# Two more blocks of the first token span in split products, with a new order table

## The chip, the cores and the metric

The kernel runs on one core of one Trainium2 chip. The metric is the time of one execution on the device in microseconds; three runs of the kernel before gave 891.29, 891.6 and 891.9 us.

## The reference

The reference is an attention with linear cost, followed by a gated feed-forward layer, all in fp32. With B = 8, H = 8, S = 576 tokens and D = 64 the second part sees 4608 tokens of width 512, and DF = 1536.

```python
q_s = exp(q - max(q, axis=-1));  q_s = q_s / (sum(q_s, axis=-1) + 1e-9)
k_s = exp(k - max(k, axis=2));   k_s = k_s / (sum(k_s, axis=2) + 1e-9)
kv  = einsum('bhsd,bhse->bhde', k_s, v)
x   = einsum('bhsd,bhde->bhse', q_s, kv)       # then tokens x (heads * D)
out = (sigmoid(x @ w_gate) * (x @ w_val)) @ w_out
```

The two input weight matrices come as `w_in`, cut into 12 blocks of 128 columns of each, the output weights as `wo`, in 12 blocks of 128 rows. Both arrive as 64-bit floats and are narrowed to fp32 on the chip, in four steps that the names `w_top`, `w_low`, `w_sign`, `w_join` (and `wo_...`) stand for: ScalarE converts the upper words, VectorE shifts the lower ones, ScalarE casts the sign, VectorE joins the bits.

## The kernel before, in words

The tokens are taken in nine spans of 512. In spans 1 to 8 (`g1`, `g2`) the product with `w_in` goes over six pairs of blocks, in a scheme with seven products for each 2x2 of sub-blocks; its right sides are the weights of a pair, kept on the chip as `a_w`, and four sums of their parts, kept in memory as `s`. Each fp32 number there is split in a high and a low part of fewer bits (`fp32r`), and a product is the sum of high x high, high x low and low x high.

The first span is another: here the weights are still being read, narrowed, summed (`w_sums`, `sums_keep`) and split (`split_hi` on ScalarE, `split_lo` on VectorE) while the span is computed block by block. For block j, `g1_0(j)` makes gate and value into two PSUM banks, `g_sig_0` and `g_mul_0` make h from them, and `g2_0(j)` multiplies h with the output block into four accumulators. Blocks 0 to 5 take `g1_0` in plain fp32 from the narrowed weights `f_w` and `x_0`; blocks 6 to 11 take it as split products from `a_w`, `a_21` and `x_hl`. `g2_0` is plain fp32 for blocks 0 to 4 and split for 5 to 11 (`in_parts`), with `h_hi_0` and `h_lo_0` for h and `wo_hi`, `wo_lo` for the output weights. An output block is stored for the later spans in both parts (`wo_store`, 512 KB) or, where `wo_late` says so, whole (`wo_keep`, 256 KB), and is then split in the second span (`wo_load` into a staging tile, `wo_split`, and a store).

Beside the blocks of the first span runs the attention for the second: the maxima of batch 1's keys (`k_max_turn` on TensorE, `k_max_send`, `k_max_read`), their subtraction (`k_sub`, five instructions `ring<-ring,kmax_b` on VectorE), exponentials, `k_mm`, and the like for the queries. `k_max_send` is a copy on ScalarE into `kmax_b` and a small transfer of 2 KB to memory (`kmax_row`); `k_max_read` is a transfer that spreads the row over 128 partitions, back into `kmax_b`. Both are issued by GpSimd, the second when the first has landed. Loads are issued by SyncE.

Every engine works off its own instructions in the order in which the program wrote them. From the first load to the start of span 2's second pair that order isn't the code's: the class `Steps` keeps the calls under the name of their step, and `put(ORDER)` writes them out as the table `ORDER` lists them (the line of all of these is then L89; L87 is the line of a call outside the table). What waits for what follows from the tiles that the instructions share.

Of the kernel before, what the change touches and what calls it, by code (L numbers as in the profile page):

```python
# [99 lines left out]
qf_tr.0.0 q_sum_0.2:1 qT_copy.0 q_sum_0.2:2 qf_tr.0.1 top:15 top:16 qT_copy.1 k_done_0 k_done_0:1 w_top.0.1  # L100
qf_mul.0.2 x_mm_0.0 kv_split.0:2 qf_mul.0.3 x_ev_0.0 w_low.0.0 qf_tr.0.2 x_mm_0.1 qT_copy.2 top:17 w_low.0.1
top:18 qf_tr.0.3 x_mm_0.2 qT_copy.3 w_join.0.0 x_mm_0.3 x_ev_0.2 x_ev_0.1 wo_top.0 w_top.1 wo_low.0 x_ev_0.3
wo_sign.0 w_join.0.1 w_low.1 split_hi.0 w_sign.1 split_lo.0 w_join.1 g1_0.0 g_sig_0.0 wo_join.0 wo_top.1
w_sums.0 load_wo.3 load_w.4 k_load.1.3 w_top.2 g_mul_0.0 wo_low.1 kv_split.0:3 w_sums.0:1 w_low.2 top:19
w_sign.2 x_split_hi.0 g1_0.1@4 g_sig_0.1 w_sums.0:2 w_top.3 g1_0.1 k_max_turn.1 g_mul_0.1 wo_hi.0 w_join.2
wo_sign.1 wo_top.2 qn_max.1.0 kv_split.0 w_low.3 g2_0.0 wo_low.2 w_sign.3 wo_join.1 qn_sub.1.0 load_wo.4
kT_load.2.1 k_load.1.1 v_load.1.1 wo_sign.2 k_load.1.4 load_w.5 qn_max.1.3 k_max_send.1 qn_max.1.2
k_max_send.1:1 qn_max.1.1 wo_join.2 qn_sub.1.2 g1_0.2@4 g_sig_0.2 load_wo.5 k_load.1.2 v_load.1.0 load_w.6
k_load.1.0 w_join.3 k_max_read.1 sums_keep.0 qn_sub.1.3 k_sum.1.3 load_w.7 x_split_lo.0 g1_0.2 k_sum.1.0
wo_top.3 qn_sub.1.1 wo_hi.1 wo_low.3 kv_split.0:1 k_sum.1.1 wo_lo.0 w_top.4 g2_0.1 x_split_hi.1 w_low.4  # L110
top:20 qn_exp.1.3 qn_exp.1.0 qn_sum.1.3 split_hi.1:1 g_mul_0.2 split_hi.0:1 k_sub.1.1 wo_sign.3 k_sum.2.0
wo_join.3 w_sign.4 w_sums.0:3 wo_keep.3 load_wo.6 v_load.1.4 v_load.1.2 v_load.1.3 qn_sum.1.0 sums_keep.0:1
w_sums.1 split_hi.1 wo_store.0 wo_lo.1 g1_0.3 w_join.4 wo_store.1 wo_top.4 sums_keep.0:3 k_sum.1.2 k_sub.1.4
sums_keep.1 load_w.8 qn_exp.1.2 sums_keep.0:2 wo_low.4 w_top.5 qn_sum.1.2 wo_keep.2 top:21 g2_0.2 qn_exp.1.1
# [1628 lines left out]
```

## Time and profile before

| | |
|---|---|
| median of three runs | 891.6 us |
| profiled execution, its time | 891.47 us |
| its span in the trace | 889.7 us |
| TensorE busy | 880.2 us (99%) |
| VectorE busy | 710.5 us (80%) |
| ScalarE busy | 592.1 us (67%) |
| GpSimd busy | 174.5 us (20%) |
| granted clock of TensorE, mean | 0.998 |

The span is what the trace shows from the first to the last instruction; 1.8 us of the execution's time lie around it. Shares are means over stages with different limits: what a change in one stage is worth is read from that stage.

### The profile page before, as it was taken

To read this page: it belongs to the slowest core of one execution; us is meant where nothing else is said; L and a number is where in the kernel's file an instruction comes from. 1 tells how busy PE (TensorE), PEld (TensorE's weight loads), DVE (VectorE), ACT (ScalarE), POOL (GpSimd) and SP (SyncE) were. 2 spreads that over 40 slices of the span, in tenths; PEclk is the share of its full clock that TensorE was granted. 3 is DMA by queue.
4 is the path that set the end of the run, shared out by engine and by line. 5 is a ranking of instruction groups with operands and counts; after the bars stand their busy time and mean duration, and the time that the engine had idled before them with its cause. 6 is when DMAs were issued, how large, how long until landed. Compare 5 with 4: busy or idle time off the path is not lost.

```text
span 889.7 us, 17035 instructions
## 1 busy us (share of the span) xinstructions
PE 880.2 (99%) x6533; PEld 800.6 (90%) x6533; DVE 710.5 (80%) x1126; ACT 592.1 (67%) x1006; POOL 174.5 (20%) x326
## 2 busy tenths in 40 slices
PE   8999999999999999999999999999999999999998
PEld 7445889999999999999999999999999999999997
DVE  7889999978797788868887888878877787886553
ACT  5889877776585767676676668556856664764432
POOL 0021221312112212121212122112211212122220
PEclk9999999999999999999999999999999999999999
DMA  9798657786787579774987499648965578535441
GB/s 332 283 390 303 242 194 227 239 265 198 260 256 224 179 226 283 231 215 143 331 243 238 123 321 295 176 156 287 300 177 165 155 217 247 164 121 190 145 141 71
DMA packets 75657, 199.16 MB, mean 224 GB/s; under 512 B 12636, under 2 KB 12920, under 8 KB 74168
## 3 DMA queue, kind: packets, MB, share of 16 engines
q0 software_dynamic: 31888, 109.60, 39.3%
q1 hardware_dynamic: 43688, 88.47, 30.8%
q8 instruction: 51, 0.84, 0.4%
q14 instruction: 30, 0.25, 0.1%
HBM read 174.98 MB, written 23.05 MB: 223 GB/s over the span
## 4 chain that ended last, share of the span: by engine, by line
PE 80%; DVE 8%; DMA 7%; issue 3%; ACT 1%; POOL 0%; SPq 0%; DVEq 0%; ACTq 0%; POOLq 0%
PE gv L87 44%; PE acc L87 25%; PE gv L89 5%; PE acc L89 3%; DMA s<-s 2%; PE at L87 2%; DMA kmax_b<-kmax_row 1%; DMA out<-x 1%; DVE ring L89 1%; DMA s_sb<-s 1%; DVE s L89 1%; DMA lent<-q_in 1%; PE at L89 1%; DVE f_w L89 1%; DMA kmax_row<-kmax_b 1%
## 5 line engine op out<-in xcount | busy, mean ns | idle before, releaser
L87 PE MATMUL gv<-c_hl,s_sb 128*128 128x256 f32 x1968 | 234.1, 275 | 0.1
L87 PEld LDWEIGHTS gv<-c_hl,s_sb 128*128 128x128 f32 x1968 | 226.8, 192 | 0.4 <-DVE s_sb L87 0.3
L87 ACT COPY sg<-gv 128x512 f32<-128x512 f32 x164 | 96.1, 586 | 138.1 <-PE gv L87 136.7
L87 PE MATMUL gv<-c_hl,a_w 128*128 128x256 f32 x1476 | 185.1, 275 | 0.0
L87 PEld LDWEIGHTS gv<-c_hl,a_w 128*128 128x128 f32 x1476 | 174.8, 192 | 0.1
L87 POOL DMA_DIRECT2D s_sb<-s x160 | 86.6, 541 | 260.7 <-PE gv L87 196.1
L87 DVE TENSOR_TENSOR s_sb<-s_sb 128x512 fp32r<-128x512 f32 x162 | 106.2, 686 | 31.9 <-ACT s_sb L87 31.8
L87 DVE TENSOR_TENSOR sg<-sg 128x512 f32<-128x512 f32 (+1 forms) x123 | 70.1, 598 | 66.6 <-ACT sg L87 66.6
L87 PEld LDWEIGHTS acc<-wo_t,h 128*128 128x128 f32 x548 | 103.3, 189 | 14.6
L87 PE MATMUL acc<-wo_hl,h 128*128 128x512 f32 x504 | 116.2, 380 | 0.0
L87 PE MATMUL acc<-wo_t,h 128*128 128x512 f32 (+1 forms) x548 | 115.9, 362 | 0.0
L87 ACT CAST s_sb<-s_sb 128x512 fp32r<-128x512 f32 x162 | 98.1, 624 | 6.9 <-DMA s_sb<-s 6.4
L87 PEld LDWEIGHTS acc<-wo_hl,h 128*128 128x128 f32 x504 | 92.1, 189 | 11.6
L87 DVE TENSOR_TENSOR sg<-gv,sg 128x512 f32<-128x512 f32 (+1 forms) x123 | 73.7, 599 | 26.7 <-PE gv L87 25.3
L87 ACT ACTIVATE sg<-sg 128x512 f32<-128x512 f32 x82 | 38.4, 514 | 38.7 <-DVE sg L87 38.6
L87 DVE TENSOR_TENSOR h<-sg,h 128x1024 fp32r<-128x1024 f32 x41 | 50.3, 1226 | 1.4
L87 POOL DMA_DIRECT2D wo_hl<-wo x40 | 21.5, 536 | 149.9 <-PE acc L87 149.9
L87 ACT ACT_TABLE_LOAD x34 | 43.6, 1283 | 0.6
L89 PE MATMUL gv<-x,f_w 128*128 128x512 f32 x96 | 42.1, 593 | 0.0
L89 PE MATMUL gv<-c_hl,s_sb 128*128 128x256 f32 x336 | 40.9, 277 | 1.2 <-ACT sg L89 0.9
L87 ACT ACTIVATE ring<-ring 128x512 f32<-128x512 f32 (+1 forms) x73 | 41.0, 622 | 0.1
L89 PEld LDWEIGHTS gv<-c_hl,s_sb 128*128 128x128 f32 x336 | 39.1, 192 | 1.7 <-ACT sg L89 1.1
(207 smaller groups left out, 1244.1 us busy)
## 6 DMA issues: line engine op xcount, KB each, us to landing
s_sb<-s POOLq DMA_DIRECT2D x184, 256.0 KB, 4.9
wo_t<-wo POOLq DMA_DIRECT2D x45, 512.0 KB, 4.6
wo_hl<-wo POOLq DMA_DIRECT2D x44, 512.0 KB, 3.7
out<-x SPq DMA_DIRECT2D x35, 256.0 KB, 4.9
ring<-k_in SPq DMA_DIRECT2D x28, 256.0 KB, 8.6
ring<-qn_in SPq DMA_DIRECT2D x28, 256.0 KB, 5.0
ring<-qT_in SPq DMA_DIRECT2D x28, 256.0 KB, 5.8
q_b<-q_m_row SPq DMA_DIRECT2D x56, 128.0 KB, 6.9
```

Source lines behind the costliest of these rows:

```text
L87: do(*args, **kw)
L89: self.steps.keep(self.name, lambda: do(*args, **kw))
```

## The change

Blocks 4 and 5 of the first span take gate and value as split products, and block 4's output product is split too. For that pair 2's weights are split before their use instead of after it, and in block 5's case a third part (`THIRD`, the tile `a_21`) is made. Output block 4 is stored in both parts, blocks 0 and 1 are kept whole and split in the last step of the second span, staged in the two tiles of `v_two`. The table `ORDER` is another in nearly all of its lines and goes on for one more pair of span 2.

```diff
     def wo_late(j):
-        return 2 <= j <= 4
+        return j < 4
...
             if w == 1 and wo_late(j):
-                wo_stage[j] = x = kmax_b if i else f_last[:, 3].rearrange("p n e -> p (n e)")
+                wo_stage[j] = x = v_two[i] if p == 0 else kmax_b if i else f_last[:, 3].rearrange("p n e -> p (n e)")
...
     def in_parts(j):
-        return j >= 5
+        return j >= 4
...
-                if j < 6:
+                if j < 4:
                     pairs = [(w[:, kt // 2, sl], x_0[:, kt])]
...
-    splits = {2: (0, FIRST, LAST), 4: (1, FIRST, LAST), 5: (2, FIRST, LAST)}
+    splits = {2: (0, FIRST, LAST), 4: (1, FIRST, LAST)}
...
         ahead = ()
-        if j >= 5:
+        if j >= 3:
             ahead = (FIRST,) if j % 2 else (THIRD, LAST)
         split_hi((j + 1) // 2, ahead)
...
-            if (w, at) == (2, 1):
+            if (w, at) == (2, 2):
                 nc.put(ORDER)
...
-            if w == 1 and at == 3:
-                wo_split(w, p)
-            if w == 1 and at == 4:
+            if w == 1 and at in (4, 5):
                 wo_split(w, p)
...
-qn_exp.1.1 qn_max.1.2 k_max_send.1:1 qn_max.1.1 wo_join.2 qn_sub.1.2 g1_0.2@4 g_sig_0.2 load_wo.5 k_load.1.2 v_load.1.0 load_w.6
+qn_exp.1.1 qn_max.1.2 k_max_send.1:1 wo_top.3 split_lo.1 sums_keep.0:3 qn_exp.1.0 k_sum.1.2 qn_sub.1.2
```

**First place: blocks 3 to 5 on TensorE.** Before, from block 3's gate and value to the key products behind block 4's output product (`f_w` are fp32 weights, `acc` the output, `at` the key products):

```order
L89 MATMUL gv<-x_149,f_w 128x512 x8
L89 MATMUL acc<-wo_t,h_228 128x512 x4
L89 MATMUL gv<-x_149,f_w 128x512 x8
L89 MATMUL acc<-wo_t,h_235 128x512 x4
L89 MATMUL gv<-x_149,f_w 128x512 x8
L89 MATMUL acc<-wo_t,h_247 128x512 x4
L89 MATMUL at<-v_115,ring 64x64 x8
```

The same stretch of the changed kernel:

```order
L89 MATMUL gv<-x_149,f_w 128x512 x8
L89 MATMUL acc<-wo_t,h_226 128x512 x4
L89 MATMUL gv<-x_hl,a_w 128x512 x24
L89 MATMUL acc<-wo_t,h_233 128x512 x4
L89 MATMUL gv<-x_hl,a_245 128x512 x6
L89 MATMUL gv<-x_hl,a_w 128x512 x6
L89 MATMUL gv<-x_hl,a_245 128x512 x6
L89 MATMUL gv<-x_hl,a_w 128x512 x6
L89 MATMUL acc<-wo_hl,h_parts 128x512 x12
L89 MATMUL at<-v_115,ring 64x64 x8
```

Two times eight fp32 products became two times 24 split ones, and block 4's four output products became twelve; the rest of TensorE's order in the first span is as before.

**Second place: the key maxima on ScalarE.** Before, the copy into `kmax_b` stands behind the sign cast of weight block 3 (`x_112<-f_w`) and of output block 1:

```order
L89 ACTIVATE wo_t<-wo_raw 128x512
L89 CAST kv_sb<-f_last 64x4x64
L89 CAST x_112<-f_w 128x2x512
L89 CAST wo_raw<-wo_t 128x2x256
L89 COPY kmax_b<-at 4x128
L89 ACTIVATE h_228<-gv 128x512
```

Now it stands behind the sigmoid of block 2 (`h_226`), the sign casts of weight blocks 4 and 5 (one row, x2) and two exponentials of keys (`lent,k_sum`):

```order
L89 ACTIVATE h_226<-gv 128x512
L89 ACT_TABLE_LOAD
L89 ACTIVATE lent,k_sum<-lent,k_neg 128x576
L89 ACTIVATE f_w<-w_raw 128x1024
L89 CAST w_raw<-f_w 128x2x512 x2
L89 ACTIVATE lent,k_sum<-lent,k_neg 128x576
L89 COPY kmax_b<-at 4x128
```

It moved behind seven instructions that came after it or were elsewhere before. On VectorE, the subtraction that needs the result came, before, behind these rows (the first of them ends when the copy on ScalarE has been made for some time):

```order
L89 TENSOR_TENSOR x_hl<-x_149,x_hl 128x1024
L89 TENSOR_TENSOR ring<-ring,q_m 128x512
L89 TENSOR_SCALAR wo_raw<-wo_raw 128x2x256
L89 TENSOR_TENSOR kv_sb<-f_last,kv_sb 64x4x64
L89 TENSOR_TENSOR wo_hl<-wo_t,wo_hl 128x512
L89 TENSOR_SCALAR w_raw<-w_raw 128x2x512
L89 TENSOR_REDUCE k_neg<-kt_117 128x1
L89 TENSOR_REDUCE q_r<-ring 128x8
L89 TENSOR_TENSOR h_228<-gv,h_228 128x512
L89 TENSOR_TENSOR ring<-ring,kmax_b 128x512
```

Now these stand between the shift of block 5's words (`TENSOR_SCALAR w_raw<-w_raw`, with one row `TENSOR_TENSOR a_w<-f_w,a_w 128x512` behind it, both just ahead of the first row here) and the subtraction:

```order
L89 SCALAR_TENSOR_TENSOR f_w<-f_w,w_raw 128x1024
L89 TENSOR_TENSOR h_226<-gv,h_226 128x512
L89 TENSOR_REDUCE q_m<-ring 128x8
L89 TENSOR_TENSOR a_w<-f_w,a_w 128x2x512
L89 TENSOR_TENSOR ring<-ring,q_m 128x512
L89 TENSOR_SCALAR wo_raw<-wo_raw 128x2x256
L89 TENSOR_REDUCE q_r<-ring 128x8
L89 SCALAR_TENSOR_TENSOR f_w<-f_w,w_raw 128x1024
L89 TENSOR_TENSOR s_254<-f_w 128x512
L89 TENSOR_TENSOR a_w<-f_w,a_w 128x2x512
L89 TENSOR_TENSOR a_w<-f_w,a_w 128x512
L89 TENSOR_TENSOR ring<-ring,kmax_b 128x512 x2
```

The subtraction has kept its place among the steps of block 3, while the copy on ScalarE that it depends on went back behind weight block 5's cast.

**Third place: GpSimd's queue.** The two transfers of the maxima were the first in it; now it begins with stores of weight sums (`s_121`, `s_122`) and of output block 0 (`wo_127`):

```order
L89 DMA s_121<-s_211 128x512
L89 DMA wo_127<-wo_t 128x512
L89 DMA s_122<-s_243 128x512
L89 DMA s_121<-s_209 128x512
L89 DMA kmax_row<-kmax_b 4x128
L89 DMA s_121<-s_212 128x512
L89 DMA kmax_b<-kmax_row 128x512
L89 DMA wo_128<-wo_t 128x512
```

Four stores went ahead of the row, one between the two, and the store of output block 1 stands behind.

## Rows read from the trace of the kernel before

**Rows 1.** Busy time by stage: window, length, then busy us (instructions) by engine.

```profile
core 0: us, PE busy (x) PEld busy (x) DVE busy (x) ACT busy (x) POOL busy (x), PEclk, DMA share, GB/s
25.00:62.70 37.70, 37.70 (x90) 16.57 (x89) 32.48 (x48) 31.39 (x47) 5.10 (x9) 1.00 0.87 325
62.70:86.60 23.90, 23.90 (x134) 11.77 (x132) 23.66 (x37) 22.67 (x30) 3.84 (x8) 1.00 0.85 312
86.60:143.50 56.90, 56.18 (x283) 48.08 (x280) 53.64 (x84) 45.93 (x66) 11.55 (x19) 1.00 0.70 240
143.50:260.00 116.50, 115.36 (x924) 110.29 (x925) 97.93 (x159) 82.96 (x143) 25.82 (x48) 1.00 0.74 231
```

**Rows 2.** Timeline of TensorE: start us, busy us, merged instructions, first span.

```profile
42.13 7.03 PE L89 MATMUL gv<-x,f_w 128*128 128x512 f32 x16
48.99 3.60 PE L89 MATMUL acc<-wo_t,h 128*128 128x512 f32 x8
52.43 7.03 PE L89 MATMUL gv<-x,f_w 128*128 128x512 f32 x16
...
80.02 3.60 PE L89 MATMUL acc<-wo_t,h 128*128 128x512 f32 x8
...
86.58 5.43 PE L89 MATMUL gv<-x_hl,a_w 128*128 128x512 f32 x24
91.84 2.75 PE L89 MATMUL acc<-wo_hl,h_parts 128*128 128x512 f32 x12
94.44 0.79 PE L89 MATMUL at<-ring,kv_sb 128*128 128x64 f32 x5
...
96.15 1.69 PE L89 MATMUL gv<-x_hl,a 128*128 128x512 f32 x6
...
101.56 2.99 PE L89 MATMUL acc<-wo_hl,h_parts 128*128 128x512 f32 x12
```

**Rows 3.** Chain that ended last (start, us); then quickest landings, 100 to 200 us.

```profile
44.28 5.12 DMA kmax_row<-kmax_b
...
49.70 7.18 DMA kmax_b<-kmax_row
...
158.28 4.30 DMA kmax_b<-kmax_row
...
DMA to landing us min/median/max: 3.3/3.9/4.4
```

**Rows 4.** VectorE: timeline, groups by form (count, mean ns), and its waits.

```profile
26.36 0.69 DVE L89 COPY x<-acc 128x512 f32<-128x512 f32 x1
...
35.07 2.54 DVE L89 TENSOR_REDUCE k_neg<-lent 128x4 f32<-128x2304 f32 x1
...
56.90 0.69 DVE L89 TENSOR_TENSOR ring<-ring,kmax_b 128x512 f32<-128x512 f32 x1 [1.81 <-DMA kmax_b<-kmax_row]
57.51 0.69 DVE L89 SCALAR_TENSOR_TENSOR wo_t<-wo_t,wo_raw 128x512 int32<-128x512 int32 x1
58.11 0.69 DVE L89 TENSOR_TENSOR s<-f_w,s 128x512 f32<-128x512 f32 x1
...
60.51 1.22 DVE L89 SCALAR_TENSOR_TENSOR f_w<-f_w,w_raw 128x1024 int32<-128x1024 int32 x1
61.65 0.68 DVE L89 TENSOR_TENSOR ring<-ring,kmax_b 64x512 f32<-64x512 f32 x1
...
L89 DVE TENSOR_SCALAR wo_raw<-wo_raw 128x512 uint32<-128x512 uint32 x6 | 2.5, 422 | 1.6 <-ACT wo_t L89 1.6
...
DVE s L89 <- DMA s<-s: 2.4, 3, 1.2
...
DVE a_w L89 <- ACT a_w L89: 0.5, 1, 0.5
```

**Rows 5.** Timeline of ScalarE, with idle time ahead of a row and its releaser.

```profile
17.04 0.68 ACT L89 ACTIVATE f_w<-w_raw 128x512 f32<-128x512 f32 x1 [1.85 <-DMA w_raw<-w_in]
...
43.74 0.24 ACT L89 COPY kmax_b<-at 4x128 f32<-4x128 f32 x1
...
47.67 0.78 ACT L89 ACTIVATE lent<-lent,k_neg 128x576 f32<-128x576 f32 x1
...
66.02 1.36 ACT L89 CAST w_raw<-f_w 128x1024 f16<-128x1024 f32 x1
```

More of the change, by code (lines that the diff above doesn't have):

```diff
@@ L100 @@
[L100 to L114, printed above, removed]
@@ L190 @@
[L190 to L194 removed]
+top:7 load_w.3 load_wo.2 qn_load.1.0 qn_load.1.1 qn_load.1.2 qn_load.1.3 top:8 top:10 top:9 top:11 k_sum.0.0
@@ new lines @@
+top:17 qT_copy.3 w_join.0.0 x_ev_0.0 x_mm_0.3 x_ev_0.2 w_join.0.1 w_top.1 x_ev_0.3 load_w.4 x_split_hi.1
+w_low.1 wo_low.0 x_split_lo.1 wo_sign.0 w_sign.1 split_hi.0 w_join.1 w_sums.0:2 load_w.5 w_sums.0 g1_0.0
+sums_keep.0:2 g_sig_0.0 w_sums.0:1 w_top.2 w_sums.0:3 x_split_hi.0 wo_join.0 w_low.2 wo_keep.0 load_wo.3
+k_load.1.0 g_mul_0.0 top:19 g1_0.1@4 g_sig_0.1 w_sign.2 split_lo.0 w_top.3 g1_0.1 wo_top.2 w_low.3
+k_max_turn.1 wo_low.2 w_sign.3 w_join.2 split_hi.0:1 w_join.3 load_w.6 k_load.1.3 kv_split.0 g2_0.0
@@ new lines @@
+qn_max.1.0 split_hi.1:1 qn_max.1.1 wo_top.1 qn_max.1.3 wo_sign.2 wo_low.1 split_hi.1 wo_join.2 qn_sub.1.0
+wo_sign.1 load_wo.5 k_load.1.2 g_mul_0.1 w_top.4 wo_join.1 g1_0.2@4 g_sig_0.2 split_lo.1:1 load_wo.4
+v_load.1.0 k_load.1.1 k_load.1.4 kT_load.2.0 load_w.7 kT_load.2.1 v_load.1.4 v_load.1.2 w_low.4 v_load.1.3
+qn_sub.1.1 k_sum.1.1 qn_sub.1.3 g1_0.2 w_top.5 w_sums.1:2 x_split_lo.0 sums_keep.1:2 w_sign.4 sums_keep.0
+w_low.5 split_lo.0:1 w_sign.5 w_join.4 g2_0.1 k_sum.1.3 g_mul_0.2 load_w.8 v_load.1.1 k_max_send.1
@@ new lines @@
+split_lo.2.6.5 wo_keep.2 wo_low.5 top:20 k_exp.1.4 qn_sum.1.0 g1_0.4 wo_sign.5 k_sub.1.1 k_exp.1.3
+w_sums.1:1 k_exp.1.2 wo_join.5 k_exp.1.0 wo_join.4 kv_split.0:2 g2_0.3 qn_sum.1.3 wo_hi.4 w_join.6 k_sum.2.0
+w_top.7 qn_sum.1.3:1 load_w.9 w_sums.1:3 load_wo.8 load_wo.7 load_w.10 g_mul_0.4 sums_keep.1:3 k_exp.1.1
+w_sums.2 wo_keep.3 h_hi_0.4 kv_split.0:1 wo_hi.5 sums_keep.1:1 w_low.7 sums_keep.2 wo_lo.4 sums_keep.2:2
+w_sign.7 h_lo_0.4 g1_0.5 k_done.1:1 top:21 split_hi.3.0 qn_sum.1.3:2 qf_mul.1.0 k_sum.2.1 split_lo.3.0
@@ new lines @@
+g2_0.4 wo_lo.5 k_mm.1.0 g_sig_0.5 w_join.7 k_mm.1.1 k_mm.1.2 g_mul_0.5 k_mm.1.3 k_mm.1.4 h_hi_0.5 k_done.1:2
+qf_tr.1.0 w_sums.2:1 kv_split.1:2 kv_split.1 kv_split.0:3 sums_keep.2:1 split_hi.3.6.5 qf_mul.1.1 wo_store.4
+split_hi.3.6.5:1 w_sums.3 wo_top.6 w_sums.2:3 qT_split.1.0 h_lo_0.5 sums_keep.2:3 g1_0.6@12 g_sig_0.6
+qT_split.1.0:1 wo_store.5 w_top.8 kv_split.1:3 split_lo.3.6.5 g1_0.6 wo_low.6 w_sums.3:1 wo_sign.6
+kv_split.1:1 w_top.9 qf_mul.1.3 split_lo.3.6.5:1 g2_0.5 wo_join.6 w_low.8 x_mm.1.0@4 qn_load.2.0 x_mm.1.0
@@ new lines @@
+load_wo.9 qf_tr.1.1 qf_mul.1.2 w_sign.8 w_sums.3:2 g_mul_0.6 x_ev.1.0 sums_keep.3:2 w_low.9 h_hi_0.6
+w_join.8 g1_0.7@12 g_sig_0.7 wo_hi.6 w_sums.3:3 load_w.11 qT_split.1.1 wo_lo.6 sums_keep.3:3 wo_top.7
+sums_keep.3 qT_split.1.1:1 g1_0.7 wo_top.8 wo_store.6 wo_low.7 w_top.10 h_lo_0.6 sums_keep.3:1 g_mul_0.7
+split_hi.4.0 g2_0.6 wo_sign.7 split_lo.4.0 w_sign.9 x_mm.1.1 wo_low.8 qf_tr.1.2 w_low.10 h_hi_0.7 w_join.9
+qT_split.1.2 wo_join.7 w_sums.4:2 load_wo.10 g1_0.8@12 g_sig_0.8 qT_split.1.2:1 wo_hi.7 split_hi.4.6.5
@@ new lines @@
+wo_lo.7 wo_sign.8 h_lo_0.7 g1_0.8 x_ev.1.1 g_mul_0.8 wo_join.8 qn_max.2.0 load_wo.11 wo_hi.8 k_load.2.0
+qn_load.2.2 kT_load.2.3 qn_load.2.1 kT_load.2.2 w_sums.4 wo_top.9 g2_0.7 split_lo.4.6.5 sums_keep.4
+split_hi.4.6.5:1 w_sums.4:1 x_mm.1.2 wo_store.7 h_hi_0.8 qf_tr.1.3 split_lo.4.6.5:1 sums_keep.4:2
+qT_split.1.3 w_sums.4:3 x_ev.1.2 wo_lo.8 w_sign.10 sums_keep.4:3 sums_keep.4:1 wo_low.9 qn_sub.2.0
+wo_store.8 wo_sign.9 w_join.10 g1_0.9@12 g_sig_0.9 w_top.11 h_lo_0.8 qT_split.1.3:1 split_hi.5.0 g1_0.9
@@ new lines @@
+c_subs w_low.11 split_lo.5.0 w_sign.11 g2_0.8 wo_join.9 w_join.11 wo_hi.9 x_mm.1.3 x_ev.1.3 w_sums.5
+split_hi.5.6.5 g_mul_0.9 wo_top.10 c_subs:1 split_hi.5.6.5:1 w_sums.5:2 c_split_hi.0 wo_lo.9 g1_0.10@12
+g_sig_0.10 wo_top.11 split_lo.5.6.5:1 wo_store.9 h_hi_0.9 wo_low.10 split_lo.5.6.5 wo_sign.10 g1_0.10
+h_lo_0.9 v_load.2.4 qn_load.2.3 k_load.2.1 wo_join.10 wo_low.11 w_sums.5:1 g_mul_0.10 g2_0.9
+split_hi.5.2.3.4 top:22 wo_sign.11 w_sums.5:3 wo_hi.10 wo_join.11 sums_keep.5:3 v_load.2.3 split_hi.5.1
@@ new lines @@
+wo_lo.10 split_hi.5.2.3.4:2 wo_load.1.4:1 g1_0.11@12 g_sig_0.11 c_split_lo.0 h_hi_0.10 top:23 g1_0.11@6
+c_split_hi.5 c_subs:3 h_lo_0.10 g1_0.11 c_split_hi.3 k_max_turn.2 k_max_send.2 c_split_lo.3 c_split_hi.1
+k_max_send.2:1 c_subs:2 sums_keep.5 split_hi.5.2.3.4:1 c_split_lo.1 sums_keep.5:2 c_split_hi.2 g2_0.10
+split_lo.5.2 c_split_hi.4 split_lo.5.1 wo_hi.11 g1.1.5.4 c_split_lo.2 g1.1.5.4:1 wo_lo.11 k_load.2.4
+c_split_hi.6 g1.1.5.4:2 g_mul_0.11 s_load.4.0 split_lo.5.3 c_split_lo.5 g1.1.5.4:4 g1.1.5.4:5 s_load.4.1
@@ new lines @@
+g1.1.4.3:4 g1.1.4.3:5 s_load.3.1 s_split.4.2:1 k_sum.2.3 qn_sub.2.2 g1.1.4.3:6 g1.1.4.3:3 kT_load.3.1
+k_sub.2.4 qn_send.2.m qn_sub.2.1 g1.1.4.3:8 g1.1.4.3:7 g1.1.4.3:9 s_load.3.2 acc_out.0:4 g1.1.4.3:10
+k_exp.2.4 g1.1.4.3:11 g1.1.4.3:12 s_load.3.3 s_split.3.0 q_spread.2.m.3 qT_load.2.1 k_load.2.3 v_load.2.1
+acc_out.0:6 q_spread.2.m.2:1 q_spread.2.m.0:1 q_spread.2.m.1:1 k_load.2.2 q_spread.2.m.1 g1.1.4.3:14
+acc_out.0:2 s_split.3.0:1 g1.1.4.3:16 g1.1.4.3:13 qn_sum.2.0 s_split.3.1 g1.1.4.3:17 qT_load.2.2 v_load.2.0
@@ new lines @@
+v_load.2.2 s_split.3.2 q_spread.2.m.0 q_spread.2.m.3:1 g1.1.4.3:19 g1.1.4.3:15 g2.1.0@12 wo_load.1.4
+k_sub.2.1 g1.1.4.3:18 h_split.1.4 k_sum.2.2 h_split.1.4:1 s_split.3.3 g2.1.0 kT_load.3.0 k_done.2
+s_split.3.1:1 qn_sub.2.3 g1.1.3.2 g1.1.3.2:1 s_split.3.2:1 qn_exp.2.1 k_sub.2.3 qn_exp.2.2 g1.1.3.2:2
+s_split.3.3:1 s_load.2.0 g1.1.3.2:3 qn_sum.2.1 g1.1.3.2:4 k_done.2:1 qT_load.2.3 top:25 g1.1.3.2:5
+s_load.2.1 qT_load.2.0 q_spread.2.m.2 k_exp.2.1 k_sub.2.2 g1.1.3.2:6 qn_sum.2.2 k_exp.2.2 g1.1.3.2:7
@@ new lines @@
+k_sub.2.0 g1.1.3.2:8 g1.1.3.2:9 k_exp.2.3 k_exp.2.0 g1.1.3.2:11 g1.1.3.2:12 s_load.2.3 s_load.2.2
+g1.1.3.2:10 wo_load.1.3 g1.1.3.2:14 wo_load.1.3:1 k_mm.2.0 g1.1.3.2:13 k_mm.2.1 s_split.2.0 k_mm.2.2
+g1.1.3.2:15 k_mm.2.3 g1.1.3.2:18 g1.1.3.2:17 k_mm.2.4 s_split.2.3 g1.1.3.2:16 s_split.2.1 g1.1.3.2:19
+k_done.2:2 h_split.1.3 s_split.2.3:1 qn_exp.2.3 s_split.2.1:1 s_split.2.0:1 h_split.1.3:1 g2.1.1 g1.1.2.1
+g1.1.2.1:1 s_split.2.2 kv_split.2:2 g1.1.2.1:2 s_load.1.0 g1.1.2.1:3 kv_split.2:3 s_split.2.2:1 g1.1.2.1:4
@@ new lines @@
+h_split.1.2:1 qT_exp.2.0 s_split.1.1 g2.1.2 s_split.1.2:1 s_split.1.1:1 g1.1.1.0 g1.1.1.0:1 qT_sub.2.2
+wo_split.1.1 q_spread.2.r.2 q_spread.2.r.0:1 acc_out.0:7 q_spread.2.r.3 g1.1.1.0:2 q_spread.2.r.2:1
+q_spread.2.r.3:1 k_sum.3.1 acc_out.0:3 s_load.0.0 wo_split.1.1:1 g1.1.1.0:3 s_split.1.3:1 kT_load.3.3
+acc_out.0:5 acc_out.0:1 g1.1.1.0:4 qT_mul.2.1 g1.1.1.0:5 s_load.0.1 qT_split.2.1 g1.1.1.0:6 g1.1.1.0:7
+qT_exp.2.2 qT_split.2.1:1 g1.1.1.0:8 g1.1.1.0:9 s_load.0.2 wo_split.1.1:3 wo_load.1.0 g1.1.1.0:10
@@ new lines @@
+wo_load.1.0:1 g1.1.1.0:11 qT_mul.2.0 s_load.0.3 wo_split.1.1:4 g1.1.1.0:14 top:26 wo_split.1.1:5 g1.1.1.0:15
+g1.1.1.0:16 g1.1.1.0:18 wo_split.1.1:2 g1.1.1.0:19 g1.1.1.0:12 qT_mul.2.2 g1.1.1.0:13 qT_split.2.0
+g1.1.1.0:17 s_split.0.0 qT_mul.2.3 qT_split.2.2 qT_split.2.0:1 qT_split.2.3 qT_split.2.2:1 g2.1.3
+s_split.0.0:1 x_mm.2.0 h_split.1.1 qT_split.2.3:1 x_ev.2.0 x_mm.2.1 s_split.0.2 x_ev.2.1 x_mm.2.2
+s_split.0.1 s_split.0.2:1 wo_split.1.0 x_mm.2.3 h_split.1.1:1 s_split.0.1:1 g1.1.0 g1.1.0:1 top:27 x_ev.2.2
@@ new lines @@
+c_split_hi.0:1 x_ev.2.3 g1.1.0:2 c_subs:4 g1.1.0:3 wo_split.1.0:1 g1.1.0:4 g1.1.0:5 c_subs:5 wo_split.1.0:2
+s_split.0.3 c_subs:6 c_split_hi.2:1 g1.1.0:6 s_split.0.3:1 c_split_lo.0:1 g1.1.0:8 k_max_turn.3 g1.1.0:9
+c_subs:7 c_split_hi.1:1 g1.1.0:11 k_max_send.3 wo_split.1.0:3 g1.1.0:12 k_max_send.3:1 g1.1.0:7
+c_split_hi.4:1 g1.1.0:14 c_split_lo.1:1 g1.1.0:13 g1.1.0:10 c_split_hi.5:1 k_load.3.3 qn_load.3.3
+c_split_lo.2:1 g1.1.0:16 c_split_hi.3:1 g1.1.0:19 k_load.3.4 k_load.3.1 qn_load.3.1 qn_load.3.2 g1.1.0:17
@@ L195 @@
+qn_sum.3.0 qn_sum.3.1 qT_load.3.2 qT_load.3.3 kT_load.4.0 kT_load.4.1
 """
@@ L486, in w_sums @@
         s_32[p] = t = [four.tile([P, 1, DM], F32, name="s_32", tag="q_b") for _ in range(4)]
+        eng = nc.vector
         def tt(o, x, y, op):
-            nc.vector.tensor_tensor(out=t[o][:, 0], in0=x, in1=y, op=op)
+            eng.tensor_tensor(out=t[o][:, 0], in0=x, in1=y, op=op)
         tt(S1, f[:, 2], f[:, 3], ALU.add)
```

118 lines of the change are left out of this document (34 added, 84 removed).

## The prediction

> **What bounds the kernel now.** I read the stages first, then the engine that is full, then the engine that is full behind it. The table of stages [rows 1] shows TensorE busy for all of 25 to 62.7 us and of 62.7 to 86.6 us, and 56.18 of the 56.90 us after that: in the first span the kernel is as long as TensorE's work. In the same rows VectorE is busy 32.48 of 37.70 us, then 23.66 of 23.90 us, then 53.64 of 56.90 us. So there is a second engine with hardly any room just behind the first, and the question of this case is whether it can follow when TensorE becomes shorter. From 143.5 to 260 us TensorE idles 1.14 us and VectorE 18.6 us; there is room there.
>
> **The change, part by part.**
>
> *TensorE's products.* In order of time [rows 2], an fp32 block starts at 42.13 and the next thing at 48.99: 6.86 us. A block of split products with an even number (24 products) goes from 86.58 to 91.84: 5.26 us; one with an odd number from 96.15 to 101.56: 5.41 us. Block 4 becomes the first kind (1.60 us saved), block 5 the second (1.45). The output product of an fp32 block goes from 48.99 to 52.43 (3.44 us), the split one from 91.84 to 94.44 (2.60): block 4's saves 0.84; block 5's was split already. Sum: 3.89 us.
>
> *Start of the span.* ScalarE converted the first half of block 0's weights at 17.04, in an idle stretch of 1.85 us [rows 5]; now both halves stand behind two copies, ahead of the copies that block 0 waits for, and the first output weights with them, while a split of kv is gone from there. The cost to block 0's start is between nothing and one such conversion (0.68); I take 0.2, since the one that is gone makes up for most. Left: 3.7 us.
>
> *Work that is added to VectorE.* A third part of pair 2 (the a_245 row), the low part of block 4's h, the low part of block 4's output weights; gone from the first span are the low parts of output blocks 0 and 1. Net one instruction of 128x512, 0.60 us from start to start [rows 4]. ScalarE has the same exchange, and is busy less than VectorE in each of the three stages. It has no price of its own while neither is late; what it costs comes out of the walk below.
>
> *The moved wait: the maximum of the keys.* Batch 1's key maxima go ScalarE copy, a small transfer to memory (kmax_row), a transfer back that spreads them (kmax_b), then VectorE's subtractions. Before, the copy ended at 43.98 [rows 5], the row took 5.12 us, the spread 7.18, and VectorE, which had come to the first subtraction 1.81 us too early, began it at 56.90 [rows 3, 4]: 12.9 us from copy to subtraction. Now the order puts the copy on ScalarE behind the two sign casts of weight blocks 4 and 5 and one exponential. The second cast can't start before VectorE's shift of block 5's words. Behind that shift VectorE has 12 instructions up to the first subtraction: 7 of 0.60, 4 of 1.14 and a short one of 0.4 [rows 4]: 9.2 us. ScalarE needs at least 1.36 + 0.78 + 0.24 = 2.4 us for cast, exponential and copy [rows 5]. So VectorE arrives some 6.8 us after the copy. The transfers need 12.9 us at the pace of before. At the quickest pace of the trace (a row in 3.3, a spread in 4.30 [rows 3], and 0.3 us ahead of each) they need 8.2. In GpSimd's queue, where the row was first, four stores now stand ahead of it; the one that is ready last waits for a sum that VectorE writes before that shift, so they are out when the copy is made, and cost nothing. VectorE then stands still for 1.4 to 6.1 us, with everything queued behind the subtraction: among it the product of gate and value for block 3, block 5's third part, block 4's output weights and h. I take 3.5, nearly the middle: the row falls into loads of weights that are still running, as before, but the spread comes when they are nearly through, since blocks 4 and 5 are now loaded ahead of the keys.
>
> The Trainium skill (DMA: Bandwidth & Descriptors, Anatomy of one DMA) gives a transfer that GpSimd issues about 2.0 us and its bytes at 436 GB/s; by that the pair would take some 4.6 us, an estimate, and VectorE would not wait at all. The 5.12 and 7.18 us of this trace speak against it here [rows 3].
>
> *Does VectorE's halt reach TensorE?* From its copy of x at 26.36 [rows 4] VectorE has 73 instructions up to the low part of block 4's h: 50 of 0.60 us, 11 of 1.14, one of 2.54, six of 0.42, and five shorter than 0.75 which I put at 2.0 together. That is 49.6 us, so 76.6 without a halt if the first starts 0.60 after the copy did, and 77.1 with one of 0.5, as before, for ScalarE's casts [rows 4]. TensorE comes to block 4's output product at 80.02 - 1.60 - 1.45 + 0.2 = 77.2 [rows 2]; the low part of h is read by the last third of its 12 products, 1.7 us later, at 78.9. So VectorE may stand still for 1.8 us for nothing; the rest of the halt is TensorE's. With 3.5 us this costs 1.7. From there to block 6's output product VectorE has 35 instructions, 20.8 us by the same sizes; TensorE's stretch was 21.54 us (80.02 to 101.56) and is 0.84 shorter: 20.7 us. There is no slack left in it, and any wait of VectorE counts. In the whole first span it waits 2.4 us for stores of the weight sums [rows 4]; being late hides a part. I take 0.7 us, with 0 and 1.4 as ends. Behind it the order leaves TensorE more work per VectorE work, and nothing more is lost.
>
> *Loads, stores, the later steps.* Output blocks 0 and 1 are kept as 256 KB instead of stored as 512, block 4 the other way round; blocks 0 and 1 are split in the last step of the second span, two instructions on each of ScalarE and VectorE, where VectorE has the 18.6 us of idle time; the extra step in the table only takes the order from the table instead of the code. The 1.14 us by which TensorE idles from 143.5 to 260 [rows 1] is what a better order could win there; a worse one could lose as much. I take 0.
>
> *Sum:* 3.7 - 1.7 - 0.7 = 1.3 us less than the profiled execution's 891.47, which is 0.13 below the median of the runs shown: 890.2 us, for a median too.
>
> **The rivals.**
> *The full gain.* The maxima come back quickly, or VectorE arrives later than I count, so that it stands still for less than 1.8 us, and the stores don't make it wait. For it: the quick pair of transfers of the second span (8.2 us would leave 1.4 us of halt), and the rule of fixed cost above would bring it about too. Against it: the pace of the very transfers that move. Time: 891.47 - 3.7 = 887.8.
> *VectorE becomes the bound and the kernel slower.* The transfers keep the 12.9 us of before, so that the halt is 6.1 us: 4.3 us reach block 4's output product, and the stretch to block 6's costs the full 1.4. Net 2.0 us slower: 893.5. It decides from a halt of 4.8 us on, where the gain with 0.7 behind it is used up. For it: the same pair of transfers in the same kind of traffic. Against it: the loads ahead of it start earlier.
> *The products don't get shorter.* That can't be here: both kinds of block stand in the trace, in the same span and on the same engine.
>
> **How the numbers follow.** A measurement of this kernel tells a change from none at about 0.2%, 1.8 us. Forecast (halt of 2.5 to 5 us, result 889 to 891.5): 0.50. Full gain (887 to 889): 0.34. Slower: 0.16. The full gain is below 889.7 throughout, and 0.06 of the forecast with it: faster 0.40. The rival that ends slower passes 893.3 with 0.14, and 0.02 come from the forecast with a worse order later: slower 0.16. Same: 0.44. The range for 8 in 10 goes from the full gain's 887.8 to 893.0, just short of the slower rival's value. The forecast's own is 889.0 to 891.5.
>
> **What the profile would show.** Right: split blocks 4 and 5 at 5.3 and 5.4 us each, and block 4's output product in 2.6; a halt of VectorE ahead of its first subtraction of kmax_b, named as a wait for kmax_row's way back, of 2.5 to 5 us, at about 60 us; TensorE idle 1 to 2 us ahead of or in block 4's output product, put down to h_parts or wo_hl. Block 6's first product then starts some 2 us earlier than 86.58. Wrong, towards the full gain: TensorE without idle time from 62 to 90 us and block 6 at 82.9. Wrong, towards slower: a halt of 5 us and more, block 6 not before 86.6, and VectorE busy without a gap from there to 140 us. What would upset the sum altogether is a wait that no row of before has: ScalarE held up by the stored output weights of block 1, whose buffer block 4's conversion takes over, or TensorE waiting in the steps from 143 to 260 us, which the new order arranges anew.

## The result, and the profile after

The change made the kernel slower: 895.17 us (median of 5 runs) against 891.29, a ratio of 1.0054 with a 95% interval of 1.0036 to 1.0072. The forecast was 890.2, with a range up to 893.0. The profiled execution took 894.84 us, its span 893.0.

The stages of the changed kernel, in the columns of [rows 1]:

```profile
25.00:62.70 37.70, 37.70 (x93) 17.25 (x92) 32.54 (x43) 34.08 (x47) 5.48 (x9) 1.00 1.00 374
62.70:86.60 23.90, 20.47 (x154) 15.51 (x153) 22.39 (x39) 18.87 (x27) 4.47 (x7) 1.00 0.58 208
86.60:143.50 56.90, 53.05 (x262) 45.69 (x260) 52.37 (x82) 46.02 (x67) 12.42 (x21) 1.00 0.68 240
143.50:260.00 116.50, 115.20 (x931) 110.37 (x931) 97.51 (x159) 82.07 (x142) 25.51 (x47) 1.00 0.76 233
```

TensorE was without idle time in the second stage before and now idles 3.43 us in it; in the third it idles 3.85 us instead of 0.72. VectorE, in the third stage, is busy less than before, 52.37 us against 53.64: part of the time it stands and waits. The DMA share of the first stage rose from 0.87 to 1.00.

TensorE's timeline shows where:

```profile
60.88 5.74 PE L89 MATMUL gv<-x_hl,a_w 128*128 128x512 f32 x24
68.59 3.70 PE L89 MATMUL acc<-wo_t,h 128*128 128x512 f32 x8 [1.97 <-DVE h L89]
...
78.78 1.13 PE L89 MATMUL acc<-wo_hl,h_parts 128*128 128x512 f32 x4 [1.31 <-ACT h_parts L89]
80.06 1.99 PE L89 MATMUL acc<-wo_hl,h_parts 128*128 128x512 f32 x8 [0.15 <-DVE wo_hl L89]
...
85.03 5.43 PE L89 MATMUL gv<-x_hl,a_w 128*128 128x512 f32 x24
...
93.07 1.13 PE L89 MATMUL acc<-wo_hl,h_parts 128*128 128x512 f32 x4 [0.89 <-DVE h_parts L89]
...
96.10 0.46 PE L89 MATMUL at<-ring,kv_sb 128*128 128x448 f32 x1 [1.26 <-DVE kv_sb L89]
...
100.51 1.56 PE L89 MATMUL gv<-x_hl,a 128*128 128x512 f32 x6 [0.93 <-DVE v L89]
```

Blocks 4 (60.88) and 5 are split products as announced. But there are two groups of waits: three up to block 4's output product, 1.97 + 1.31 + 0.15 = 3.43 us, and behind block 6's start at 85.03 another 3.84 us (0.89, 1.26 and 0.93 here; 0.29 at 105.39 and 0.47 at 131.30). All of them are for something that VectorE makes, or that ScalarE makes from it.

VectorE's timeline shows what held it, and the chain of what ended last shows the transfers behind that:

```profile
56.24 0.69 DVE L89 TENSOR_TENSOR s<-f_w 128x512 f32<-128x512 f32 x1
56.85 1.82 DVE L89 TENSOR_TENSOR a_w<-f_w,a_w 128x1024 fp32r<-128x1024 f32 x2
64.17 1.29 DVE L89 TENSOR_TENSOR ring<-ring,kmax_b 128x512 f32<-128x512 f32 x2 [5.51 <-DMA kmax_b<-kmax_row]
...
88.87 0.69 DVE L89 TENSOR_TENSOR s<-f_w 128x512 f32<-128x512 f32 x1 [0.98 <-DMA s<-s]
91.72 0.69 DVE L89 TENSOR_TENSOR s<-f_w,s 128x512 f32<-128x512 f32 x1 [2.16 <-DMA s<-s]
```

```profile
52.00 6.32 DMA kmax_row<-kmax_b
58.60 5.54 DMA kmax_b<-kmax_row
...
79.94 11.68 DMA s<-s
```

These rows point to two causes, which the experiments take apart. One is the halt that the prediction speaks of, 5.51 us (1.81 before, [rows 4]). The other it priced at 0.7 us: VectorE writes new sums of weights into four buffers that take turns, and waits 0.98 and 2.16 us until old sums have been stored from them. One of those stores took 11.68 us to land.

To compare executions I use one length: from the first product of the first span's block 0 to the first product of span 2's first pair. It leaves out the start, where the granted clock from 10 to 25 us was 0.89 in some executions (before among them) and 1.00 in others (the changed kernel among them), which moves block 0 by some 1.5 us. Before it goes from 24.85 to 140.10, after from 23.33 to 141.87. The last column of the table is its first part, up to the first product of block 6: there the changed kernel is level with before, although its products are shorter, and the 3.3 us by which its first span is longer lie behind block 6.

| kernel | median, us (runs) | ratio to before, 95% | first span, us | up to block 6, us |
|---|---|---|---|---|
| before | 891.29 (5) | | 115.25 | 61.73 |
| changed | 895.17 (5) | 1.0054 (1.0036 to 1.0072) | 118.54 | 61.70 |
| 1: changed, maxima early | 890.81 (11) | 1.0000 (0.9988 to 1.0012) | 114.07 | 57.47 |
| 2: before, maxima late | 894.58 (6) | 1.0049 (1.0037 to 1.0062) | 119.05 | 65.41 |
| 3: before, maxima early | 889.95 (12) | 0.9995 (0.9984 to 1.0007) | 114.31 | 61.61 |
| 4: 1 and two stores earlier | 887.27 (12) | 0.9963 (0.9948 to 0.9977) | 110.80 | 57.47 |
| 5: 1 and three loads later | 887.32 (6) | 0.9961 (0.9946 to 0.9975) | 111.05 | 57.48 |
| 6: changed, two stores earlier | 892.47 (10) | 1.0020 (1.0005 to 1.0034) | 115.21 | 61.74 |
| 7: changed, six loads later | 892.77 (10) | 1.0025 (1.0011 to 1.0040) | 115.81 | 58.81 |
| 8: changed, row sent by ScalarE | 895.31 (4) | 1.0061 (1.0043 to 1.0078) | 118.86 | 61.90 |
| 9: 1, stores and loads | 887.37 (5) | 0.9962 (0.9950 to 0.9975) | 110.40 | 57.47 |

Each ratio compares with executions of before on the same chip, whose medians were 891.37 (runs 1 to 3), 891.31 (4 to 6) and 890.50 (7 to 9), and not with the first row, so medians and ratios can differ a little.

### The profile page after: what moved, and what is told of

The parts are those of the page before. It is cut to its first block, busy times and chain, and to the rows that moved or that the text cites. A ratio compares the mean times of both kernels' runs of the same rounds, so it can differ in the third digit from the quotient of the medians.

```text
span 893.0 us, 17080 instructions
## 1 busy us (share of the span) xinstructions
PE 874.9 (98%) x6553; PEld 803.3 (90%) x6553; DVE 710.3 (80%) x1128; ACT 592.4 (66%) x1008; POOL 178.0 (20%) x327
## 4 chain that ended last, share of the span: by engine, by line
PE 73%; DVE 9%; DMA 7%; issue 5%; ACT 5%; POOL 1%; SPq 0%; POOLq 0%; DVEq 0%; ACTq 0%
PE gv L87 41%; PE acc L87 23%; PE gv L89 4%; PE acc L89 2%; PE at L87 2%; DMA s_sb<-s 2%; DMA s<-s 1%; DMA f_last<-v_in 1%; DVE sg L89 1%; DVE c_hl L89 1%; DVE s L89 1%; DMA kmax_row<-kmax_b 1%; DVE ring L89 1%; PE at L89 1%; DVE f_w L89 1%
## 5 line engine op out<-in xcount | busy, mean ns | idle before, releaser
L87 ACT COPY sg<-gv 128x512 f32<-128x512 f32 x160 | 93.7, 586 | 137.6 <-PE gv L87 136.3
L87 PE MATMUL gv<-c_hl,a_w 128*128 128x256 f32 x1440 | 180.6, 275 | 0.0
L87 PEld LDWEIGHTS gv<-c_hl,a_w 128*128 128x128 f32 x1440 | 170.5, 192 | 0.1
L87 DVE TENSOR_TENSOR s_sb<-s_sb 128x512 fp32r<-128x512 f32 x158 | 103.6, 687 | 32.0 <-ACT s_sb L87 32.0
L87 PEld LDWEIGHTS acc<-wo_t,h 128*128 128x128 f32 x535 | 101.0, 189 | 14.1
L87 PE MATMUL acc<-wo_hl,h 128*128 128x512 f32 x492 | 113.5, 381 | 0.0
L87 PE MATMUL acc<-wo_t,h 128*128 128x512 f32 (+1 forms) x535 | 113.1, 362 | 0.0
L87 ACT CAST s_sb<-s_sb 128x512 fp32r<-128x512 f32 x158 | 95.5, 625 | 7.0 <-DMA s_sb<-s 6.9
L87 ACT ACTIVATE ring<-ring 128x512 f32<-128x512 f32 (+1 forms) x69 | 38.8, 622 | 0.1
L87 POOL DMA_DIRECT2D wo_t<-wo x39 | 21.2, 544 | 80.3 <-PE acc L87 42.5
```

Of the source, the lines that this page charges most:

```text
L87: do(*args, **kw)
```

## The experiments

All edits but one move names in the table `ORDER`; nothing is left out of the computation in any of them.

**1. The changed kernel with the key maxima sent early.**

```diff
 split_hi.0:1 w_join.3 load_w.6 k_load.1.3 kv_split.0 g2_0.0
+k_max_send.1 k_max_send.1:1 k_max_read.1
 qn_max.1.0 split_hi.1:1
...
 g2_0.1 k_sum.1.3 g_mul_0.2 load_w.8 v_load.1.1
-k_max_send.1
 qn_exp.1.1 qn_max.1.2
-k_max_send.1:1
 wo_top.3 split_lo.1
...
 wo_low.3
-k_max_read.1
 qn_sum.1.1 wo_keep.1
```

> The changed kernel, with ScalarE's copy of the key maxima and the two transfers behind it (kmax_row, kmax_b) moved up by some 10 us, to just after the maxima are turned; nothing else moves. Theory H (the halt of VectorE ahead of the first ring<-ring,kmax_b, 5.51 us in the changed kernel, is what costs, with the lateness of stores and of h that follows it up to 143 us): the halt goes to 0, TensorE's idle time from 62.7 to 143.5 us falls from 7.3 us to under 3, and the time is 889 to 891 us, 4 to 6 below the changed kernel. Rival V (VectorE has no room for the split of blocks 4 and 5 at all; the halt only shows where it is short): the halt goes, VectorE's idle time appears further on at other waits, and the time stays at 893 to 895. Rival S (the stores of the sums, s<-s, are too late whatever the maxima do): 2 to 3 us of waits for s<-s stay near 89 and 92 us, 892 to 893.

The halt is gone and the first span is 4.47 us shorter than the changed kernel's, 4.23 of it up to block 6; the median fell by 4.4, as theory H said. Block 6, and the stages from 62.7 us on:

```profile
82.24 5.43 PE L89 MATMUL gv<-x_hl,a_w 128*128 128x512 f32 x24
```

```profile
62.70:86.60 23.90, 23.90 (x173) 19.43 (x172) 22.86 (x39) 22.24 (x34) 6.26 (x9) 1.00 0.75 283
86.60:143.50 56.90, 53.31 (x275) 46.13 (x275) 53.22 (x83) 44.56 (x64) 11.85 (x21) 1.00 0.64 221
```

TensorE is full again in the first of them, but still idles 3.59 us in the second, more than H allowed. VectorE's waits (us in total, times, longest) say what is left:

```profile
DVE s L89 <- DMA s<-s: 4.0, 3, 2.4
```

These are 0.79 us at 58 us, where TensorE is full, and 0.85 and 2.40 us at 86 and 89 us. So the halt explains the first group of waits and not the second; that part of rival S is right.

**2 and 3. The kernel before with the maxima late, and early.**

```diff
 load_w.5 qn_max.1.3
-k_max_send.1
 qn_max.1.2
-k_max_send.1:1
 qn_max.1.1 wo_join.2
...
 k_load.1.0 w_join.3
-k_max_read.1
 sums_keep.0 qn_sub.1.3 k_sum.1.3
+k_max_send.1 k_max_send.1:1 k_max_read.1
 load_w.7 x_split_lo.0
```

Run 3 takes the three names from the same places and puts them behind `g2_0.0`, as run 1 does.

> The kernel of before, with the same copy and the two transfers moved down by some 4.7 us (behind the sigmoid of block 2 and one exponential of the keys); nothing else moves. VectorE's halt there grows from 1.81 to about 6.5 us. Theory H: the halt alone costs about 3 to 4.5 us of the 4.7 added, so 894 to 896. Rival V: before has no split of blocks 4 and 5, so VectorE has room to take it in, and the time rises by less than 1.5, to 891 to 892.5.

> The kernel of before, with ScalarE's copy of the key maxima moved up by one place, ahead of the cast x<-f_w, so that the two transfers start some 1.8 us earlier and VectorE's halt of 1.81 us closes. It shows whether the prediction was right that this much of a halt is free: if it is, the time stays within 0.5 us of 891.3; if the halt of before was paid for, it falls by 1 to 1.8 us, to 889.5 to 890.3.

Late, the row left 3.2 us after its time in the kernel before (47.52 against 44.28 us), not the 4.7 of the expectation; VectorE's halt is 5.34 us instead of the expected 6.5, and TensorE waits for weights and then for h:

```profile
59.13 0.69 DVE L89 TENSOR_TENSOR ring<-ring,kmax_b 128x512 f32<-128x512 f32 x1 [5.34 <-DMA kmax_b<-kmax_row]
```

```profile
64.02 3.70 PE L89 MATMUL gv<-x,f_w 128*128 128x512 f32 x8 [2.59 <-DVE f_w L89]
68.38 3.70 PE L89 MATMUL gv<-x,f_w 128*128 128x512 f32 x8 [0.67 <-ACT h L89]
```

So 3.5 us more of halt cost 3.3 us of TensorE's time and 3.8 us of first span in a kernel without the new split products: the price belongs to the halt, not to VectorE's added work (rival V expected less than 1.5). Early (the row left at 40.19 us, 4.1 earlier and not 1.8), the halt is gone, and block 6 comes 61.61 us after block 0 instead of 61.73. So the 1.81 us of halt before had cost next to nothing there; the rest of the 0.94 us by which this first span is shorter lies behind block 6. The median, 889.95, is one that the expectation gave to a halt that was paid for, but against before on the same chip the ratio of 0.9995 (0.9984 to 1.0007) can't be told from no change.

**4. Run 1 with two stores of sums moved up.** The third sum of pair 2 is written near 57 us, but its store stands behind those of later sums and of an output block in GpSimd's queue; the second sum of pair 1 likewise.

```diff
 w_sums.2:2
+sums_keep.2:2
 split_hi.2.6.5:1
...
 w_sums.1:1
+sums_keep.1:1
 k_exp.1.2
...
 kv_split.0:1 wo_hi.5
-sums_keep.1:1
 w_low.7 sums_keep.2 wo_lo.4
-sums_keep.2:2
 w_sign.7
```

> The changed kernel with the key maxima sent early (as in the first run of this study), and two stores of sums moved up on GpSimd's queue to where their sums are ready: the third sum of block pair 2 (written at 58.4 us, stored only at 77.5) and the second of pair 1 (written at 69.7, stored at 76.5). Theory H, second part (what is left between 86 and 143 us, 3.6 us of TensorE's idle time, comes from VectorE's two waits for s<-s of 0.85 and 2.40 us near 86 and 89 us, because those stores stand late in the order): the two waits go, TensorE's idle time there falls to about 1 us, and the time is 888 to 889, 2 to 3 below the 890.8 of the kernel with the maxima early. Rival V (VectorE has no room in this stage): the waits go, but the idle time of TensorE stays at 3 us or more with VectorE busy without a pause, 890 to 891. Rival D (the stores land late because 3 MB of loads are issued at 73 to 75 us): the waits stay at over 1.5 us, since the stores still run beside the loads.

```profile
62.70:86.60 23.90, 23.90 (x174) 19.43 (x173) 23.78 (x41) 22.09 (x33) 6.71 (x10) 1.00 0.82 314
86.60:143.50 56.90, 56.10 (x312) 49.74 (x311) 55.59 (x87) 46.28 (x67) 12.11 (x21) 1.00 0.62 209
```

Both waits went, and TensorE's idle time of the last stage fell from 3.59 to 0.80 us. VectorE is now busy 55.59 of 56.90 us and still follows: it had the room, if only just. The median is 887.27, a little better than H said, and faster than the kernel before by 0.37%.

**5. Run 1 with three loads later.** In the changed kernel SyncE issues 3 MB of loads just ahead of those stores:

```profile
76.45 0.33 SPq L89 DMA_DIRECT2D sg<-w_in  x1
76.87 0.86 SPq L89 DMA_DIRECT2D wo_raw<-wo_in  x2
77.78 0.76 SPq L89 DMA_DIRECT2D w_raw<-w_in  x1
```

and GpSimd its stores just behind:

```profile
77.37 0.54 POOL L89 DMA_DIRECT2D s<-s  x1 [6.24 <-DVE s L89]
77.90 0.65 POOL L89 DMA_DIRECT2D wo<-wo_t  x1
78.54 1.94 POOL L89 DMA_DIRECT2D s<-s  x3
```

```diff
 w_top.7 qn_sum.1.3:1 load_w.9 w_sums.1:3
-load_wo.8 load_wo.7 load_w.10
 g_mul_0.4
...
 x_mm.1.0@4 qn_load.2.0
+load_wo.8 load_wo.7 load_w.10
 x_mm.1.0
```

> The changed kernel with the key maxima sent early, the stores where they were, and three loads (output weights 7 and 8 and weights 10, 2 MB together) put behind the load of the next queries on SyncE's queue, so that they are issued at about 80 us and not at 74. Rival D (the stores of 76 to 78 us land late, 11.27 us, because these loads are in flight beside them): the stores land in 5 to 7 us, the waits of 0.85 and 2.40 us go, 888 to 889.5. Theory H, second part: the stores stand too late in the order in the first place; they land a little sooner, the wait of 2.40 falls by 1 to 2 us, 889 to 890.5. Either way 889.5 or less speaks against rival V.

The stores landed in 6.3 us (median of six; 9.0 in the changed kernel), as rival D said, and both waits went here too, with the stores as late in the order as they were. TensorE is busy 55.88 us of the last stage, and the time, 887.32, is that of run 4 and a little better than D's 888. So the wait needed both: stores that were issued late, and 2 MB of loads in flight beside them. Taking away either is enough.

**6. The changed kernel with the two stores moved up, the maxima late.** The edit is that of run 4, made in the changed kernel.

> The changed kernel with the key maxima as late as they are, and only the two stores of sums moved up. Theory H: the halt of 5.5 us stays and with it 3.4 us of TensorE's idle time at 68 and 79 us; the waits for s<-s near 89 and 92 us (0.98 and 2.16) shorten, so 892.5 to 894. If the stores alone were the cause (rival S), the time falls to 891 or less.

The halt stayed and with it 1.89 us of idle time ahead of block 3's output products; the waits for stores are gone, and in the last stage TensorE is busy 56.03 us.

```profile
63.96 1.29 DVE L89 TENSOR_TENSOR ring<-ring,kmax_b 128x512 f32<-128x512 f32 x2 [5.44 <-DMA kmax_b<-kmax_row]
```

First span: 3.33 us less than the changed kernel. Run 1 took away 4.47 and both together, in run 4, 7.74: the two losses add up.

**7. The changed kernel with six loads later.** Why did the maxima take so long? Here nothing else is moved than loads that SyncE issued at 48 to 54 us, shortly before the two transfers and at their start.

```diff
 kT_load.2.0 load_w.7
-kT_load.2.1 v_load.1.4 v_load.1.2
 w_low.4
-v_load.1.3
 qn_sub.1.1
...
 g_mul_0.2
-load_w.8 v_load.1.1
 k_max_send.1
...
 load_wo.6
+kT_load.2.1 v_load.1.4 v_load.1.2 v_load.1.3 load_w.8 v_load.1.1
 wo_top.4
```

> The changed kernel, with the maxima as late as they are and only six loads moved on SyncE's queue (keys and values of batch 1 and 2 and the 1 MB of weight block 8, 2.2 MB in all) behind the load of output block 6, so that they are issued at about 67 us instead of 48 to 53 and no load is started while the maxima's two transfers run (52 to 64 us). Theory T (the pair's 6.32 and 5.54 us come from the loads in flight beside them): the pair lands in 8 to 10 us together instead of 11.9, the halt of VectorE shrinks from 5.5 to 2 to 4 us, and the time falls by 1 to 2.5 us, to 892.7 to 894.2. Rival L (they are the length of such a transfer anyway): the halt stays at 5 to 5.5 us and the time at 894.5 to 896, or above if the moved loads come late.

```profile
51.99 5.03 DMA kmax_row<-kmax_b
57.31 3.79 DMA kmax_b<-kmax_row
```

```profile
61.13 1.29 DVE L89 TENSOR_TENSOR ring<-ring,kmax_b 128x512 f32<-128x512 f32 x2 [2.48 <-DMA kmax_b<-kmax_row]
```

```profile
76.02 3.14 PE L89 MATMUL acc<-wo_hl,h_parts 128*128 128x512 f32 x12 [0.79 <-ACT h_parts L89]
```

The pair took 8.8 us instead of 11.9 and the halt was 2.48, as theory T said; of that, 0.79 us reached TensorE as idle time, and block 6 came 1.34 us later than in run 1.

**8. The changed kernel with the row sent by ScalarE.**

```diff
-        (nc.sync if b > 2 else nc.gpsimd).dma_start(
+        (nc.sync if b > 2 else nc.scalar if b == 1 else nc.gpsimd).dma_start(
             out=row.rearrange("(h p) -> h p", h=NP), in_=kmax_b[:NP, 0:P]
```

> The changed kernel, with the first of the two transfers (2 KB to memory, kmax_row) issued by ScalarE right behind its copy instead of by GpSimd. Theory T: the transfer meets the same loads and lands in 5 to 6.5 us as before; the halt stays within 0.5 us of 5.5 and the time at 894.5 to 896. Rival Q (GpSimd's queue, with the stores of sums ahead of it in it, holds it): it lands in 2.5 to 4.5 us, the halt falls to 3 to 4 us and the time to 893 to 894.3.

```profile
51.78 0.52 ACTq L89 DMA_DIRECT2D kmax_row<-kmax_b  x1
```

```profile
57.23 0.55 POOL L89 DMA_DIRECT2D kmax_b<-kmax_row  x1 [7.08 <-ACT a_w L89]
```

```profile
57.23 7.03 DMA kmax_b<-kmax_row
```

GpSimd issued the way back 5.45 us after ScalarE had issued the row, against 6.60 us in the changed kernel. The trace gives no landing for the row here, and names a cast of ScalarE as what ended GpSimd's wait, so 5.45 us is the most that the row can have taken. It gained nothing: the way back started 1.4 us sooner than in the changed kernel, but took 7.03 us instead of 5.54 and landed at 64.26 instead of 64.14. In both executions the DMA share is 0.97 or more from 62 to 64 us and 0.31 or less from 64 to 66: the way back landed when the traffic beside it ended, though it was issued at different times. So the halt was 5.59 us and the time the changed kernel's, and the gain that rival Q expected from another queue for the row did not come. The way back itself stayed in GpSimd's queue; moving it was not tried. The Trainium skill (DMA: Bandwidth & Descriptors, Issuing engines are not separate DMA queues) says that whichever engine issues, the bytes go through the same 16 DMA engines. This run agrees, with the halt and the time unchanged.

**9. Stores and loads together, with the maxima early.** The edits of runs 4 and 5 on top of run 1.

> The changed kernel with the maxima sent early, the two stores of sums moved up and the three loads behind the queries' load, all together. Theory H: each of the last two closes the same waits for s<-s, so the two together give no more than one of them: 886.5 to 887.8. If loads and stores were two separate losses, a further 1 to 2 us: 885 to 886.

887.37: no more than either alone, as H said; they close the same waits.

## Why the prediction was wrong

**TensorE's saving, 3.7 us: right, and a little more.** In run 4, where hardly anything waits:

```profile
57.82 3.60 PE L89 MATMUL acc<-wo_t,h 128*128 128x512 f32 x8
60.85 5.74 PE L89 MATMUL gv<-x_hl,a_w 128*128 128x512 f32 x24
66.43 3.60 PE L89 MATMUL acc<-wo_t,h 128*128 128x512 f32 x8
69.46 1.86 PE L89 MATMUL gv<-x_hl,a 128*128 128x512 f32 x6
...
75.04 2.75 PE L89 MATMUL acc<-wo_hl,h_parts 128*128 128x512 f32 x12
77.73 1.15 PE L89 MATMUL at<-v,ring 128*64 128x64 f32 x32
...
80.77 5.43 PE L89 MATMUL gv<-x_hl,a_w 128*128 128x512 f32 x24
```

Block 4's products take 5.58 us from start to start (60.85 to 66.43), block 5's 5.58 and block 4's output product 2.69, where 5.26, 5.41 and 2.60 were put in. The fp32 output products that stand ahead of blocks 4 and 5 take 3.03 instead of 3.44 each, which the sum did not have. Up to block 6, runs 3 and 4 (before and after with the maxima early, both without idle time of TensorE there) differ by 61.61 - 57.47 = 4.14 us; over the whole first span by 3.51. The start cost nothing that shows: block 0 begins at 23.50 in run 3 and 23.30 in run 4, both at a clock of 1.00 there.

**The free part of a halt, 1.8 us: nearly right.** By TensorE's idle time it is 2.48 - 0.79 = 1.69 us in run 7 and 5.51 - 3.43 = 2.08 in the changed kernel. By how much later block 6 comes than in run 1 it is less, 1.1 and 1.3 us (2.48 - 1.34; 5.51 - 4.23): the delay is larger than the idle time, 4.23 against 3.43 us in the changed kernel.

**"I take 3.5, nearly the middle" for the halt: too small.** The two walks it rests on held: VectorE came to the subtraction 6.95 us after the copy (51.71 to 58.66; forecast 6.8), and GpSimd's stores were issued by 49.58, before the copy. What failed is the reason, that the spread comes when the loads "are nearly through": the DMA share was 1.00 while the row was on its way and 1.02 during the spread.

```profile
51.47 0.24 ACT L89 COPY kmax_b<-at 4x128 f32<-4x128 f32 x1
```

```profile
52.00:58.30 6.30, 6.30 (x17) 2.72 (x16) 6.27 (x9) 6.30 (x13) 1.06 (x2) 1.00 1.00 385
58.60:64.10 5.50, 5.50 (x21) 3.61 (x20) 0.07 (x1) 2.81 (x4) 1.61 (x3) 1.00 1.02 388
```

Copy to subtraction took 12.5 us, nearly the 12.9 of before, and the halt was 5.51. TensorE idled 3.4 us for it and block 6 came 4.2 us later than in run 1, where 1.7 was forecast. Runs 1, 2 and 7 show the size and the cause.

**"I take 0.7 us, with 0 and 1.4 as ends" for the stores, and "nothing more is lost" behind it: the second and as large a miss.** From block 6 to the end of the first span the changed kernel took 56.84 us, before 53.52: 3.3 us lost. 3.84 us of TensorE's idle time lie there, and runs 4 and 5 take away 2.8 and 2.6 of the 3.59 that run 1 had left. The walk had rightly found no slack in that stretch, but priced the store waits by what they were in [rows 4], although the order that decides when a sum is stored and which loads run beside it had been changed.

**Later steps, 0: probably some 1 us too little.** From the first pair of span 2 to the end the changed kernel took 751.13 us, before 749.60. The eight executions with the changed order there took 749.7 to 752.1, 750.9 in the mean; the three with the old one 749.6 to 750.3, 750.0 in the mean. These are single executions, so a loss of about 1 us is likely and not shown, and no run takes it apart: the longest new wait of the changed kernel (1.33 us at 300.35, for a result of ScalarE) was about 0.5 us or less in the other seven.

ScalarE's wait for the stored weights of output block 1, named as a risk, may be there: it idles 3.81 us ahead of 65.24, where it takes over their buffer, for a cause that the profile doesn't name. It lies inside the halt and was not taken apart.

So the rival that ends slower came true by its condition, transfers that keep the pace of before, with a halt above its 4.8 us. Its own price, 893.5, was still too low, mainly by the part of the store waits. What its name says did not come: VectorE was not the bound by its own work, for in run 4 it did the same work in time.
